# Mish feed-forward block on one core: x tiles 0 and 1 loaded one by one, w1's parts regrouped over two queues, tile 0 ahead of tile 1

## The chip, the core and the metric

One core of one Trainium2 chip runs the kernel. TensorE multiplies, VectorE (DVE) and ScalarE (ACT) read the products from PSUM, SyncE (SP) and ScalarE issue the DMAs, GpSimd (POOL) only builds an index table. The metric is the time of one execution on the device in microseconds (us). Three runs of the kernel before gave 105.01, 104.5 and 105.01 us, a median of 105.01.

## The reference

```python
B, S, D, F = 1, 2048, 512, 1792      # bfloat16
h = einsum("bsd,df->bsf", x, w1) + b1
sp = log1p(exp(-abs(h))) + where(h > 0, h, 0)
act = h * tanh(sp)                   # Mish
out = einsum("bsf,fd->bsd", act, w2)
```

## The kernel before

The 2048 rows of x are taken in four blocks of 512 (`BLOCKS`), a block being four tiles of 128 rows. The inner dimension D = 512 is four parts of 128, k = 0 to 3; F = 1792 is fourteen parts, f = 0 to 13. For each block the first half (`mm1`) makes, for each f, a PSUM bank of 128 x 512 from four products, one for each k, with a 128 x 128 piece of w1 as the weights and 512 columns of x transposed (`xT`) streaming; ScalarE then adds the bias, takes Mish and writes `a_sb` (`mish`, L159). The second half (`mm2`) makes, for each tile of rows, a bank from fourteen products over f; VectorE copies it to `o_sb` and SyncE stores it (`put`). Blocks go one after the other, and TensorE's order is the order in which the program is written.

There are eight banks of PSUM. In block 0, f uses bank (4 + f) % 8, so that f = 8 writes the bank that f = 0 wrote, and `mm1_step` makes TensorE wait for `free[bank]` ahead of an f's first product: there stands the token of whatever read the bank last.

Tiles of x come in two ways. Blocks 1 to 3 and tiles 2 and 3 of block 0 are transposed by the DMA on the way in (`t_xT`, `t_x23`). Tiles 0 and 1 are loaded as they lie (`x_nat`, one load of 256 rows, rows 2p and 2p + 1 in partition p) and transposed on TensorE by products with an identity (`transpose_x`, L145), copied from PSUM to `xT` by VectorE or ScalarE (L150).

The opening is what the change is about. TensorE first runs products on constants (`WARM`, L105), which need no load: 3200 columns in all. Then come the eight transposes and the first eight f of block 0 (`OPEN`), in an order written out by hand (L250 to L257): `first(fs, js, ks)` runs the products of these f, tiles js and parts k, k outermost. f 0 to 3 meet k 0 on tile 0 and then on tile 1, f 4 to 7 meet k 0 on both, then all eight f meet k 1 and 2 on tiles 0 and 1, then k 0 to 2 on tiles 2 and 3, and last k 3 on all four tiles, 512 columns wide. The last of each f starts its Mish.

Loads are issued by two engines, each in its order. ScalarE (L109): w1's part k 0, then k 2, for f 0 to 7. SyncE (L111 to L125): x's tiles 0 and 1, w1's k 1, then after a wait for the third product of `WARM` the DMA transpose of tiles 2 and 3, w1's k 3, b1, the rest of w1 (f 8 to 13), w2, and the DMA transposes of blocks 1 to 3. b1 is spread over partitions by VectorE (`spread_b1`, L246).

Of the kernel before, what the change touches and what calls it, by code (L numbers as in the profile page):

```python
# [4 lines left out]

P = 128
SQ = 32
WARM = (512,) * 5 + (256,) * 2 + (128,)
BLOCKS = (512, 512, 512, 512)


# [21 lines left out]
def bass_standalone__dense_activation_mish__prompt_kernel(  # L33
# [14 lines left out]
    KT, FT = D // P, F // P  # L48
    assert (S, D, F) == (2048, 512, 1792) and sum(BLOCKS) == S
    x2, out2 = x[0], out[0]  # L50
# [3 lines left out]
    OPEN = 8  # L54
    N0 = BLOCKS[0] // P

    with ExitStack() as es:
        def sb(name, shape, t):
            return es.enter_context(nc.sbuf_tensor(name, shape, t))

        x_nat = sb("x_nat", [P, 2, D], BF)
        xT = sb("xT", [P, KT, S], BF)
# [6 lines left out]
        ident = sb("ident", [P, P], BF)  # L69
        a_sb = sb("a_sb", [P, FT, S], BF)  # L70
        o_sb = sb("o_sb", [P, S // P, D], BF)
        ps = es.enter_context(nc.psum_tensor("ps", [P, 8, 512], F32))

        def sem(name):
            return es.enter_context(nc.semaphore(name))

        sp = Stream(nc.sync, None)
        pe = Stream(nc.tensor, sem("c_pe"))
        dve = Stream(nc.vector, sem("c_dve"))
        act = Stream(nc.scalar, sem("c_act"))  # L80
        pool = Stream(nc.gpsimd, sem("c_pool"))

        def load(q, dst, src, name, transpose=False):
            s = sem(name)
            (q.eng.dma_start_transpose if transpose else q.eng.dma_start)(dst, src).then_inc(s, 16)
            return (s, 16)

        def load_w1(q, ks, a, b):
            return load(q, w1_sb[:, ks, a * P:b * P], w1v[:, ks, a * P:b * P], "s_w1_%d_%d" % (ks.start, a))
# [6 lines left out]
        def load_part(q, k0, k1, a, b):  # L96
            t = load_w1(q, slice(k0, k1), a, b)
            for f in range(a, b):
                for k in range(k0, k1):
                    t_w1[k, f] = t  # L100

        t_bz = dve.mark(nc.vector.memset(b1_nat[:, :], 0.0))  # L102
        c_w = nc.const_aps.tensor(1.0, [P, P], BF)
        c_m = nc.const_aps.tensor(1.0, [P, 512], BF)
        t_fill = [pe.mark(nc.tensor.matmul(ps[:, 7, 0:n], c_w, c_m[:, 0:n], start=True, stop=True)) for n in WARM]  # L105

        act.eng.preload_act_table(ACT.Mish)  # L107
        act.wait(t_bz)
        for k in (0, 2):  # L109
            load_part(act, k, k + 1, 0, OPEN)  # L110
        t_xn = load(sp, x_nat[:, :, :], x2[0:2 * P, :].rearrange("(p j) d -> p j d", p=P), "s_xn")  # L111
        load_part(sp, 1, 2, 0, OPEN)
        sp.wait(t_fill[2])
        t_x23 = load(sp, xT[:, :, 2 * P:4 * P], x2[2 * P:4 * P, :], "s_x23", True)
        load_part(sp, 3, 4, 0, OPEN)
        sp.wait(t_bz)
        t_b1 = load(sp, b1_nat[0:FT, :], b1.rearrange("(j p) -> j p", p=P), "s_b1")
        load_part(sp, 0, KT, OPEN, FT)
        t = load(sp, w2_sb[:, :, :], w2v, "s_w2")
# [3 lines left out]
        for s in range(1, len(BLOCKS)):  # L123
            lo, hi = starts[s], starts[s + 1]
# [5 lines left out]
        t_id = dve.mark(nc.vector.tensor_scalar(ident[:, :], diff[:, :], 0, None, ALU.is_equal))  # L130

        free = [[] for _ in range(8)]
        t_cp = {(j, k): t_x23 for j in (2, 3) for k in range(KT)}
        t_mish = {}

        def transpose_x():

            pe.wait(t_xn, t_id)
            for bank, (eng, js, ks) in enumerate(((dve, (0,), (0,)), (act, (1,), (0,)), (dve, (0, 1), (1,)),
                                                  (act, (0, 1), (2, 3)))):  # L140
                n, m = len(ks), len(js)
                for i, k in enumerate(ks):
                    for h, j in enumerate(js):
                        lo = (i * m + h) * P
                        mm = nc.tensor.matmul(ps[:, bank, lo:lo + P], x_nat[:, j, k * P:(k + 1) * P], ident[:, :],  # L145
                                              start=True, stop=True)
                eng.wait(pe.mark(mm))
                dst = xT[:, ks[0]:ks[0] + n, js[0] * P:(js[-1] + 1) * P]
                src = ps[:, bank, 0:n * m * P].rearrange("p (k t) -> p k t", k=n)
                t = eng.mark(nc.vector.tensor_copy(dst, src) if eng is dve else act.eng.activation(dst, src, ACT.Copy))  # L150
                for k in ks:
                    for j in js:
                        t_cp[j, k] = t
                free[bank] = [t]

        def mish(s, f, bank, t_mm):
            n = BLOCKS[s]
            act.wait(t_b1c, t_mm)
            t = act.mark(act.eng.activation(a_sb[:, f, starts[s]:starts[s + 1]], ps[:, bank, 0:n], ACT.Mish,  # L159
                                            bias=b1_sb[:, f:f + 1]))  # L160
            t_mish[s, f] = t
            free[bank] = [t]

        def mm1_step(s, f, k, bank, js=None):

            n = BLOCKS[s]
            lo, hi = (0, n) if js is None else (js[0] * P, (js[-1] + 1) * P)
            first = k == 0 and lo == 0
            if first:
                pe.wait(*free[bank])  # L170
            pe.wait(t_w1[k, f])
            if s:
                pe.wait(t_xT[s])
            else:
                pe.wait(*[t_cp[j, k] for j in (js or range(N0))])
            return nc.tensor.matmul(ps[:, bank, lo:hi], w1_sb[:, k, f * P:(f + 1) * P],  # L176
                                    xT[:, k, starts[s] + lo:starts[s] + hi], start=first, stop=(k == KT - 1 and hi == n))
# [8 lines left out]

        def rows(i):

            if i < 2:
                return out2[0:2 * P, :].rearrange("(p j) d -> p j d", p=P)[:, i, :]  # L190
            return out2[i * P:(i + 1) * P, :]

        def mm2_step(i, f, lo, hi, bank):
# [7 lines left out]
        def put(i, lo, hi, bank, t_mm, q=sp):  # L201
            nonlocal n_out
            dve.wait(t_mm)
            t = dve.mark(nc.vector.tensor_copy(o_sb[:, i, lo:hi], ps[:, bank, 0:hi - lo]))  # L204
            free[bank] = [t]
            q.wait(t)
            q.eng.dma_start(rows(i)[:, lo:hi], o_sb[:, i, lo:hi]).then_inc(s_out, 16)
            n_out += 1
# [8 lines left out]
        def mm2_last(i):  # L217

            nonlocal n_out
            cuts = (0, D - 3 * P // 2, D - P // 2, D)  # L220
            toks = []
            for n, eng in enumerate((dve, dve, act)):
                lo, hi, bank = cuts[n], cuts[n + 1], (i + n) % 4
                for f in range(FT):
                    mm = mm2_step(i, f, lo, hi, bank)
                eng.wait(pe.mark(mm))
                dst, src = o_sb[:, i, lo:hi], ps[:, bank, 0:hi - lo]
                t = eng.mark(nc.vector.tensor_copy(dst, src) if eng is dve else act.eng.activation(dst, src, ACT.Copy))  # L228
# [12 lines left out]


        def spread_b1():
            dve.wait(t_b1)
            for j in range(P // SQ):
                t = dve.mark(nc.vector.transpose(b1_T[j * SQ:(j + 1) * SQ, :], b1_nat[:, j * SQ:(j + 1) * SQ]))  # L246
            dve.wait(t)
            return dve.mark(nc.vector.tensor_copy(b1_sb[:, :], b1_T[:, 0:FT]))  # L248

        transpose_x()  # L250
        t_b1c = spread_b1()
        first(range(4), (0,), (0,))
        first(range(4), (1,), (0,))
        first(range(4, OPEN), (0, 1), (0,))
        first(range(OPEN), (0, 1), (1, 2))
        first(range(OPEN), (2, 3), (0, 1, 2))
        first(range(OPEN), None, (3,), True)  # L257
        for f in range(OPEN, FT):
            mm1(0, f, (4 + f) % 8)

# [39 lines left out]
```

## Time and profile before

| | us |
|---|---|
| median of three runs | 105.01 |
| span of the profiled execution, first to last instruction | 104.0 |
| TensorE products busy | 101.4 (98% of the span) |
| weight loads busy (beside products) | 50.0 |
| ScalarE busy | 39.5 |
| VectorE busy | 13.2 |
| bytes moved by DMA | 7.94 MB |

The page gives no time of its own for the profiled execution other than the span. A busy share says how long an engine had at least one instruction under way; instructions on TensorE overlap, so that a product's duration is longer than the step from one to the next. In a row of the timeline the first number is the start in us from the span's first instruction, the second the length, then engine, line, operation, what is written and read, the shape and the count. SPq and ACTq are the DMA issues of SyncE and ScalarE; PEld is TensorE's weight load. The arrow in square brackets gives the idle time ahead of a row and what ended it. In the program's names w_sb stands for both `w1_sb` and `w2_sb`.

### The profile page before, as it was taken

To read this page: it belongs to the slowest core of one execution; us is meant where nothing else is said; L and a number is where in the kernel's file an instruction comes from. 1 tells how busy PE (TensorE), PEld (TensorE's weight loads), DVE (VectorE), ACT (ScalarE), POOL (GpSimd) and SP (SyncE) were. 2 spreads that over 40 slices of the span, in tenths; PEclk is the share of its full clock that TensorE was granted. 3 is DMA by queue.
4 is the path that set the end of the run, shared out by engine and by line. 5 is a ranking of instruction groups with operands and counts; after the bars stand their busy time and mean duration, and the time that the engine had idled before them with its cause. 6 is when DMAs were issued, how large, how long until landed. Compare 5 with 4: busy or idle time off the path is not lost.

```text
span 104.0 us, 1180 instructions
## 1 busy us (share of the span) xinstructions
PE 101.4 (98%) x520; PEld 50.0 (48%) x520; DVE 13.2 (13%) x26; ACT 39.5 (38%) x60; POOL 0.4 (0%) x5
## 2 busy tenths in 40 slices
PE   7999999999999999999999999999999999999993
PEld 2888444444444444444444444444444444444472
DVE  1212000112220000022220000022112000021241
ACT  4300899300027777200007777500005777700000
POOL 1000000000000000000000000000000000000000
PEclk9999999999999999999999999999999999999999
DMA  2999999991101000010111000001111000001111
GB/s 70 367 295 368 359 223 193 199 204 50 50 3 47 0 0 6 0 50 12 39 50 50 0 0 3 0 6 50 50 50 50 0 0 0 0 0 56 52 50 50
DMA packets 12833, 7.94 MB, mean 76 GB/s; under 512 B 7836, under 2 KB 12188, under 8 KB 12828
## 3 DMA queue, kind: packets, MB, share of 16 engines
q1 hardware_dynamic: 12396, 7.33, 26.8%
q10 hardware_dynamic: 432, 0.54, 1.5%
q8 instruction: 4, 0.07, 0.3%
q14 instruction: 1, 0.01, 0.0%
HBM read 3.94 MB, written 2.10 MB: 58 GB/s over the span
## 4 chain that ended last, share of the span: by engine, by line
PE 98%; ACT 0%; issue 0%
PE ps L176 47%; PE ps L198 47%; PE ps L105 3%; PE ps L145 1%; ACT o_sb L228 0%
## 5 line engine op out<-in xcount | busy, mean ns | idle before, releaser
L159 ACT ACTIVATE a_sb<-ps,b_sb 128x512 bf16<-128x512 f32 x56 | 37.1, 698 | 48.5 <-PE ps L176 48.5
L176 PE MATMUL ps<-xT,w_sb 128*128 128x512 bf16 (+2 forms) x252 | 50.0, 361 | 0.0
L198 PE MATMUL ps<-w_sb,a_sb 128*128 128x512 bf16 (+3 forms) x252 | 49.1, 355 | 0.0
L176 PEld LDWEIGHTS ps<-xT,w_sb 128*128 128x128 bf16 x252 | 25.0, 101 | 24.1
L198 PEld LDWEIGHTS ps<-w_sb,a_sb 128*128 128x128 bf16 x252 | 23.2, 98 | 25.6
L204 DVE CAST o_sb<-ps 128x512 bf16<-128x512 f32 x15 | 10.4, 692 | 80.8 <-PE ps L198 80.8
L228 ACT ACTIVATE o_sb<-ps 128x64 bf16<-128x64 f32 x1 | 0.2, 224 | 11.5 <-PE ps L198 11.5
L105 PE MATMUL ps<-const-bfloat16-1.0 128*128 128x512 bf16 (+2 forms) x8 | 2.8, 532 | 0.8 <-PEq L285 0.8
L105 PEld LDWEIGHTS ps<-const-bfloat16-1.0 128*128 128x128 bf16 x8 | 1.0, 136 | 2.2 <-issue 2.1
L150 ACT ACTIVATE xT<-ps 128x128 bf16<-128x128 f32 (+1 forms) x2 | 0.9, 438 | 2.2 <-PE ps L145 2.2
L107 ACT ACT_TABLE_LOAD x1 | 1.3, 1283 | 0.7 <-PEq L285 0.7
L246 DVE STREAM_TRANSPOSE b_T<-b_nat 32x32 bf16<-32x32 bf16 x4 | 0.8, 202 | 3.1 <-DMA b_nat<-in_b_dram 3.0
L145 PE MATMUL ps<-ident,x_nat 128*128 128x128 bf16 x8 | 1.0, 309 | 0.0
L150 DVE CAST xT<-ps 128x128 bf16<-128x128 f32 (+1 forms) x2 | 0.7, 358 | 2.5 <-PE ps L145 2.4
L228 DVE CAST o_sb<-ps 128x320 bf16<-128x320 f32 (+1 forms) x2 | 0.8, 392 | 1.5 <-PE ps L198 1.5
L145 PEld LDWEIGHTS ps<-ident,x_nat 128*128 128x128 bf16 x8 | 0.8, 138 | 0.2 <-DMA x_nat<-in_x_dram 0.2
L130 DVE TENSOR_SCALAR ident<-diff 128x128 bf16<-128x128 int32 x1 | 0.2, 227 | 0.2 <-POOL diff L128 0.2
L128 POOL IOTA diff<- 128x128 int32 x1 | 0.2, 234 | 0.4 <-POOLq L285 0.4
L102 DVE MEMSET b_nat<- 32x64 uint32 x1 | 0.1, 112 | 0.8 <-PEq L285 0.8
L248 DVE CAST b_sb<-b_T 128x14 f32<-128x14 bf16 x1 | 0.2, 176 | 0.0
L285 POOL MEMSET const-bfloat16-1.0<- 128x1 bf16 x1 | 0.1, 101 | 0.0
L285 POOL MEMSET const-uint8-127<- 128x1 uint8 x1 | 0.1, 101 | 0.0
(2 smaller groups left out, 0.2 us busy)
## 6 DMA issues: line engine op xcount, KB each, us to landing
out_dram<-o_sb SPq DMA_DIRECT2D x15, 128.0 KB, 1.7
w_sb<-in_w_dram SPq DMA_DIRECT2D x1, 1792.0 KB, 10.5
w_sb<-in_w_dram SPq DMA_DIRECT2D x1, 768.0 KB, 5.8
w_sb<-in_w_dram ACTq DMA_DIRECT2D x2, 256.0 KB, 3.7
w_sb<-in_w_dram SPq DMA_DIRECT2D x2, 256.0 KB, 3.6
x_nat<-in_x_dram SPq DMA_DIRECT2D x1, 256.0 KB, 2.6
out_dram<-o_sb SPq DMA_DIRECT2D x1, 112.0 KB, 1.7
xT<-in_x_dram SPq DMA_TRANSPOSE x4, 5.2
```

Of the source, the lines that this page charges most:

```text
L105: t_fill = [pe.mark(nc.tensor.matmul(ps[:, 7, 0:n], c_w, c_m[:, 0:n], start=True, stop=True)) for n in WARM]
L107: act.eng.preload_act_table(ACT.Mish)
L128: t_diff = pool.mark(pool.eng.iota(diff[:, :], pattern=[[1, P]], base=0, channel_multiplier=-1))
L130: t_id = dve.mark(nc.vector.tensor_scalar(ident[:, :], diff[:, :], 0, None, ALU.is_equal))
L145: mm = nc.tensor.matmul(ps[:, bank, lo:lo + P], x_nat[:, j, k * P:(k + 1) * P], ident[:, :], start=True, stop=True)
L150: t = eng.mark(nc.vector.tensor_copy(dst, src) if eng is dve else act.eng.activation(dst, src, ACT.Copy))
L159: t = act.mark(act.eng.activation(a_sb[:, f, starts[s]:starts[s + 1]], ps[:, bank, 0:n], ACT.Mish, bias=b1_sb[:, f:f + 1]))
L176: return nc.tensor.matmul(ps[:, bank, lo:hi], w1_sb[:, k, f * P:(f + 1) * P], xT[:, k, starts[s] + lo:starts[s] + hi], start=first, stop=( ...
L198: return nc.tensor.matmul(ps[:, bank, 0:hi - lo], a_sb[:, f, i * P:(i + 1) * P], w2_sb[:, f, lo:hi], start=(f == 0), stop=(f == FT - 1))
L204: t = dve.mark(nc.vector.tensor_copy(o_sb[:, i, lo:hi], ps[:, bank, 0:hi - lo]))
L228: t = eng.mark(nc.vector.tensor_copy(dst, src) if eng is dve else act.eng.activation(dst, src, ACT.Copy))
L246: t = dve.mark(nc.vector.transpose(b1_T[j * SQ:(j + 1) * SQ, :], b1_nat[:, j * SQ:(j + 1) * SQ]))
```

## The change

Tiles 0 and 1 become two loads of 128 rows in their plain order, both at the head of SyncE's queue; w1's k 0 and k 1 are issued by ScalarE, k 2 and k 3 by SyncE behind x; the DMA transpose of tiles 2 and 3 follows these without a wait for the warm-up. The warm-up has 2432 columns. Each tile has its own four transposes, k 0 copied by VectorE and k 1 to 3 by ScalarE in one copy, banks 0 and 1 for tile 0 and 2 and 3 for tile 1. Behind tile 0's transposes stand 384 columns on constants (`BRIDGE`), then f 0 to 3 meet k 0 on tile 0, and only then come tile 1's transposes. The order of the rest of the opening: f 4 and 5 on tile 0 and f 0 to 5 on tile 1 with k 0, f 6 and 7 on both, all f with k 1 to 3 on tiles 0 and 1, and at the end all f with k 0 to 3 on tiles 2 and 3.

```diff
-WARM = (512,) * 5 + (256,) * 2 + (128,)
+WARM = (512,) * 4 + (256, 128)
+BRIDGE = (256, 128)
...
+        def load_tile(q, j):
+            return load(q, x_nat[:, j, :], x2[j * P:(j + 1) * P, :], "s_xn%d" % j)
+
         act.eng.preload_act_table(ACT.Mish)
         act.wait(t_bz)
-        for k in (0, 2):
-            load_part(act, k, k + 1, 0, OPEN)
-        t_xn = load(sp, x_nat[:, :, :], x2[0:2 * P, :].rearrange("(p j) d -> p j d", p=P), "s_xn")
-        load_part(sp, 1, 2, 0, OPEN)
-        sp.wait(t_fill[2])
+        t_xn = [load_tile(sp, 0), load_tile(sp, 1)]
+        load_part(act, 0, 1, 0, OPEN)
+        load_part(act, 1, 2, 0, OPEN)
+        load_part(sp, 2, 3, 0, OPEN)
+        load_part(sp, 3, 4, 0, OPEN)
         t_x23 = load(sp, xT[:, :, 2 * P:4 * P], x2[2 * P:4 * P, :], "s_x23", True)
-        load_part(sp, 3, 4, 0, OPEN)
...
-        def transpose_x():
-
-            pe.wait(t_xn, t_id)
-            for bank, (eng, js, ks) in enumerate(((dve, (0,), (0,)), (act, (1,), (0,)), (dve, (0, 1), (1,)),
-                                                  (act, (0, 1), (2, 3)))):
-                n, m = len(ks), len(js)
+        def transpose_x(j):
+
+            pe.wait(t_xn[j], t_id)
+            for bank, ks, eng in ((2 * j, (0,), dve), (2 * j + 1, (1, 2, 3), act)):
+                n = len(ks)
                 for i, k in enumerate(ks):
...
-                dst = xT[:, ks[0]:ks[0] + n, js[0] * P:(js[-1] + 1) * P]
-                src = ps[:, bank, 0:n * m * P].rearrange("p (k t) -> p k t", k=n)
+                dst = xT[:, ks[0]:ks[0] + n, j * P:(j + 1) * P]
+                src = ps[:, bank, 0:n * P].rearrange("p (k t) -> p k t", k=n)
...
         def rows(i):
 
-            if i < 2:
-                return out2[0:2 * P, :].rearrange("(p j) d -> p j d", p=P)[:, i, :]
             return out2[i * P:(i + 1) * P, :]
...
-        transpose_x()
+        transpose_x(0)
+        for n in BRIDGE:
+            nc.tensor.matmul(ps[:, 7, 0:n], c_w, c_m[:, 0:n], start=True, stop=True)
+        first(range(4), (0,), (0,))
+        transpose_x(1)
         t_b1c = spread_b1()
-        first(range(4), (0,), (0,))
-        first(range(4), (1,), (0,))
-        first(range(4, OPEN), (0, 1), (0,))
-        first(range(OPEN), (0, 1), (1, 2))
-        first(range(OPEN), (2, 3), (0, 1, 2))
-        first(range(OPEN), None, (3,), True)
+        first((4, 5), (0,), (0,))
+        first(range(6), (1,), (0,))
+        first((6, 7), (0, 1), (0,))
+        first(range(OPEN), (0, 1), (1, 2, 3))
+        first(range(OPEN), (2, 3), range(KT), True)
```

More of the change, by code (lines that the diff above doesn't have):

```diff
@@ L134, in bass_standalone__dense_activation_mish__prompt_kernel @@
         t_mish = {}
-        def transpose_x():
-            pe.wait(t_xn, t_id)
-            for bank, (eng, js, ks) in enumerate(((dve, (0,), (0,)), (act, (1,), (0,)), (dve, (0, 1), (1,)),
-                                                  (act, (0, 1), (2, 3)))):
-                n, m = len(ks), len(js)
+        def transpose_x(j):
+            pe.wait(t_xn[j], t_id)
+            for bank, ks, eng in ((2 * j, (0,), dve), (2 * j + 1, (1, 2, 3), act)):
+                n = len(ks)
                 for i, k in enumerate(ks):
[L143 to L146, printed above, removed]
+                    mm = nc.tensor.matmul(ps[:, bank, i * P:(i + 1) * P], x_nat[:, j, k * P:(k + 1) * P], ident[:, :],
+                                          start=True, stop=True)
                 eng.wait(pe.mark(mm))
-                dst = xT[:, ks[0]:ks[0] + n, js[0] * P:(js[-1] + 1) * P]
-                src = ps[:, bank, 0:n * m * P].rearrange("p (k t) -> p k t", k=n)
+                dst = xT[:, ks[0]:ks[0] + n, j * P:(j + 1) * P]
+                src = ps[:, bank, 0:n * P].rearrange("p (k t) -> p k t", k=n)
                 t = eng.mark(nc.vector.tensor_copy(dst, src) if eng is dve else act.eng.activation(dst, src, ACT.Copy))
                 for k in ks:
-                    for j in js:
-                        t_cp[j, k] = t
+                    t_cp[j, k] = t
                 free[bank] = [t]
```

## The prediction

> **What bounds the kernel now.** First the chain of waits, the view that follows the end of the run back to its start. Columns: start, length, what.
>
> ```profile
> 0.77 2.82 PE ps L105 x8
> 3.60 0.85 PE ps L145 x8
> 4.45 13.01 PE ps L176 x84
> 17.46 12.09 PE ps L198 x56
> 29.55 12.09 PE ps L176 x56
> ```
>
> TensorE is the whole chain: warm-up (L105), transposes of x (L145), then products with no hole. A full half stage is 56 products of 512 columns in 12.09 us, 0.216 each, and nothing after 17.46 is touched. Block 0's first half takes 13.01, and what can be won is in there and in the 3.6 us ahead of it. Next the timeline of the opening, to see when work starts and how fast it goes.
>
> ```profile
> 1.58 1.48 PE L105 MATMUL ps<-const-bfloat16-1.0 128*128 128x512 bf16 x3
> ...
> 3.40 0.78 PEld L145 LDWEIGHTS ps<-ident,x_nat 128*128 128x128 bf16 x8 [0.18 <-DMA x_nat<-in_x_dram]
> 3.41 1.04 PE L145 MATMUL ps<-ident,x_nat 128*128 128x128 bf16 x8
> ...
> 3.74 0.74 DVE L150 CAST xT<-ps 128x128 bf16<-128x128 f32 x2 [2.42 <-PE ps L145]
> ...
> 4.25 1.06 PE L176 MATMUL ps<-xT,w_sb 128*128 128x128 bf16 x8
> ...
> 5.10 1.06 PE L176 MATMUL ps<-xT,w_sb 128*128 128x256 bf16 x4
> ...
> 6.13 1.36 PE L176 MATMUL ps<-xT,w_sb 128*128 128x256 bf16 x11
> ```
>
> The next rows group products by shape, the warm-up's of 2.2 to 2.5 us and the 256-column ones of 5.5 to 5.8 and of 6.4 to 6.7: count, busy time, mean ns of one.
>
> ```profile
> L105 PE MATMUL ps<-const-bfloat16-1.0 128*128 128x512 bf16 x3 | 1.5, 631 | 0.0
> ...
> L176 PE MATMUL ps<-xT,w_sb 128*128 128x256 bf16 x4 | 1.1, 418 | 0.0
> ...
> L176 PE MATMUL ps<-xT,w_sb 128*128 128x256 bf16 x6 | 0.8, 273 | 0.0
> ```
>
> A 256-column product takes 418 ns, then 273: at about 6.1 the array doubles its speed (the granted clock reads 1.00 on both sides, so only the durations show this). Steps from start to start: 512 columns cold (1.48 - 0.63) / 2 = 0.425; 256 cold (1.06 - 0.42) / 3 = 0.213; 128 cold 0.107 (eight from 4.25 end where 5.10 begins); 256 warm (1.36 - 0.27) / 10 = 0.109. A microsecond lost before 6.1 therefore costs half a microsecond at the end; one lost later costs all of itself. TensorE works without a break from 0.77 to 6.1, 5.3 us, before the clock rises. The tiles of x arrive (3.40) just as the warm-up ends.
>
> **The loads.** First the issues; then each load's size and its time from issue to landing, k 0, k 1 and k 3 in this order.
>
> ```profile
> 0.74 0.40 SPq L85 DMA_DIRECT2D x_nat<-in_x_dram  x1
> ...
> 0.95 0.86 ACTq L85 DMA_DIRECT2D w_sb<-in_w_dram  x2
> ...
> 1.20 0.41 SPq L85 DMA_DIRECT2D w_sb<-in_w_dram  x1
> ...
> 2.24 1.30 SPq L85 DMA_TRANSPOSE xT<-in_x_dram  x1
> ...
> 3.60 0.57 SPq L85 DMA_DIRECT2D w_sb<-in_w_dram  x1
> ```
>
> ```profile
> x_nat<-in_x_dram SPq DMA_DIRECT2D x1, 256.0 KB, 2.6
> w_sb<-in_w_dram ACTq DMA_DIRECT2D x1, 256.0 KB, 3.1
> w_sb<-in_w_dram SPq DMA_DIRECT2D x1, 256.0 KB, 3.6
> ...
> w_sb<-in_w_dram SPq DMA_DIRECT2D x1, 256.0 KB, 3.7
> ...
> xT<-in_x_dram SPq DMA_TRANSPOSE x1, 4.3
> ```
>
> And the bytes moved by stretch: the last column is GB/s.
>
> ```profile
> 1.60:2.00 0.40, 0.40 (x2) 0.13 (x1) 0.00 (x0) 0.40 (x1) 0.00 (x0) 1.00 0.59 108
> 2.00:2.40 0.40, 0.40 (x2) 0.15 (x1) 0.00 (x0) 0.02 (x1) 0.00 (x0) 1.00 0.64 200
> 2.40:2.80 0.40, 0.40 (x2) 0.15 (x1) 0.00 (x0) 0.00 (x0) 0.00 (x0) 1.00 0.96 328
> 2.80:3.20 0.40, 0.40 (x3) 0.27 (x2) 0.00 (x0) 0.00 (x0) 0.00 (x0) 1.00 0.95 343
> 3.20:3.60 0.40, 0.40 (x5) 0.22 (x4) 0.00 (x0) 0.00 (x0) 0.00 (x0) 1.00 1.06 389
> ```
>
> x lands at 0.74 + 2.6 = 3.34, k 0 at 0.95 + 3.1 = 4.05, k 1 at 1.20 + 3.6 = 4.80. Bytes moved: 43 KB by 2.0, 123 by 2.4, 254 by 2.8, 391 by 3.2, 547 by 3.6. x's 262 KB are through at 2.8, x and k 0 together (524) at 3.55, so a load's semaphore comes some 0.53 us behind its last byte. Which queue moves when is seen in the queues' shares of 3.0 to 3.4 us:
>
> ```profile
> q10 hardware_dynamic: 74, 0.15, 98.4%
> q1 hardware_dynamic: 1, 0.00, 4.0%
> ```
>
> q10 is ScalarE's, q1 SyncE's: k 0 has the engines nearly alone, though k 1 was issued on the other ring 2 us ago. With the landings 0.7 apart this reads as one load after the other in order of issue, across both rings.
>
> **The change, part by part.**
>
> *Loads.* The new order of issue is x 0 (SyncE 0.74), k 0 (ScalarE 0.95, where it was), x 1 (SyncE 1.14), k 1 (ScalarE, about 1.35), k 2 and k 3 (SyncE, 1.55 and 1.96), the DMA transpose (from about 2.4 for its 1.30), then b1 and the rest, all of which SyncE reaches some 0.4 us sooner than now since its wait on the warm-up is gone. Each 131 KB tile and each 262 KB part in turn over the byte counts above: x 0 through at 2.45, lands at 3.0; with rows half as long, which the early trace does not show, I take 3.05 (bounds: 2.8, where the warm-up ends, and 3.34, as the whole x now). x 0 and k 0 are 393 KB, through at 3.2: k 0 lands at 3.75. With x 1, 3.55: x 1 lands at 4.1. Then 0.7 each: k 1 at 4.8, k 2 at 5.5, k 3 at 6.3; the transpose, which now lands at 2.24 + 4.3 = 6.54 with k 3 behind it at 3.60 + 3.7 = 7.3, becomes the last of the same bytes, 7.3. Those that follow stay.
>
> *Warm-up.* 2432 columns in place of 3200 end at 0.77 + 2432 x 0.83 ns = 2.80. TensorE is then idle until x 0's first transpose at 3.05 + 0.05 = 3.10 (now 3.34 to 3.41).
>
> *Tile 0 first.* Four transposes 3.10 to 3.53, bridge of 384 columns 0.32, to 3.85. The copy that the first product needs is hidden by these: now it is 3.41 to 4.03 and the product needs it by 4.25, so 0.62 to 0.75 us are enough. k 0 lands at 3.75, 0.10 early. Four products of 128 columns: 3.85 to 4.28. Then tile 1's four transposes (x 1 is there since 4.1): 4.28 to 4.71; f 4 and 5 on tile 0: 4.92. Tile 1's six products of k 0 need VectorE's copy, 0.75 after 4.28, 5.03: a wait of 0.1 (bounds 0 and 0.11). Six by 0.107: 5.67. f 6 and 7 on both tiles, two by 0.213: 6.10. ScalarE's copies of k 1 to 3 (384 columns, between the two rows below) are over by 4.71 + 0.3 + 0.6 = 5.6 and free bank 3 in time.
>
> ```profile
> L150 ACT ACTIVATE xT<-ps 128x512 bf16<-128x512 f32 x1 | 0.6, 597 | 0.4 <-PE ps L145 0.4
> ...
> L150 ACT ACTIVATE xT<-ps 128x128 bf16<-128x128 f32 x1 | 0.3, 278 | 1.8 <-PE ps L145 1.8
> ```
>
> *Rest of the opening.* 24 products of k 1 to 3 on tiles 0 and 1, 32 of all k on tiles 2 and 3, 56 by 0.109 = 6.10: from 6.10, where the clock rises, to 12.20. k 1 is needed at 6.1, k 2 at 7.0, k 3 at 7.8, the transpose at 8.7: each load has 1.3 us or more to spare. The opening now has 70 products in place of 60 for the same columns; the ten more weight loads cost nothing, since the 128-column products above already run one load each at the full step of 0.107. Tiles 0 and 1 are also stored as plain rows now; the stores lie beside the later products, whose chain has no store in it, so nothing is put down for that.
>
> *The end of the opening.* Here the change adds a wait. Today:
>
> ```profile
> 10.39 0.81 PE L176 MATMUL ps<-xT,w_sb 128*128 128x512 bf16 x3
> ...
> 10.88 0.69 ACT L159 ACTIVATE a_sb<-ps,b_sb 128x512 bf16<-128x512 f32 x1 [5.79 <-PE ps L176]
> ...
> 10.88 2.42 ACT L159 ACTIVATE a_sb<-ps,b_sb 128x512 bf16<-128x512 f32 x4 [5.79 <-PE ps L176]
> ...
> 12.12 1.24 PE L176 MATMUL ps<-xT,w_sb 128*128 128x512 bf16 x5
> ```
>
> The last eight products, one for each f, are 512 wide and take 1.73 us, 10.39 to 12.12. f 0's Mish starts 0.11 behind its product's end, is over at 11.57, and so bank 4 is free 0.55 before f 8, at 12.12, writes it. After the change the last eight are 256 wide and take 0.87: they start at 12.20 - 0.87 = 11.33, f 0 is finished at 11.60, its Mish runs 11.71 to 12.40, and f 8 waits for bank 4 until 12.45 (0.05 as from x's landing to its use): 0.25 us at full price. Behind it in TensorE's order stands all the rest. f 9 needs the second Mish, (2.42 - 0.69) / 3 = 0.58 later, and comes 0.86 later, so only the first waits. All fourteen Mish end near 11.71 + 14 x 0.58 = 19.8; the second half needs the last at 12.45 + 5.18 + 2.8 = 20.4.
>
> **Sum.** The opening ends at 12.20 against 12.12, +0.08, and f 8 waits 0.25: +0.33. The shorter warm-up (0.32 us less of idle columns, worth 0.16) is eaten by the idle 0.3 before x 0, the 0.1 before tile 1 and the fine-grained order. The profiled span of 104.0 becomes 104.3. The median of the runs shown is 105.0, 1.0 above that span, which I carry over: 105.3.
>
> *A rule against the trace.* The Trainium skill (DMA: Bandwidth & Descriptors, "Queues, rings and completion order") says that each DMA engine takes turns between the rings that have work, packet by packet. The shares above show turns by whole loads instead, here. By the rule x 1 would share the engines with k 0, and the sum is that of the second rival.
>
> **Rivals.**
>
> *The first landings come late.* For: the first stretches move 108 and 200 GB/s against 389, and short rows or shared turns could keep x 0 until 3.34 and k 0 until 4.05 or 4.1. Against: the queues' shares. Then the first product starts at 3.41 + 0.75 = 4.16 in place of 3.85, 0.31 cold, 0.15 at the end: 105.45.
>
> *The clock rises later* (the other side). Place: TensorE's break from 2.80 to 3.10, where it had none. If what raises the clock counts unbroken work, it counts anew from 3.10, and 5.3 us later is 8.4: 2.3 us more at half speed, 1.15: 106.5. It decides once a break of 0.3 us counts. For: now there is no break at all ahead of the rise. Against: 0.3 in 5.3 is little, and the trace has no other break to judge by. The Trainium skill (TensorE: Matmul & The Clock Gate, "Part 1: The HAM clock gate") has free-running windows of 3.4 us of which one must be busy; by it, an estimate, the present rise would close a window begun at 2.7, and if the break spoils that one the rise moves to 9.5 and the time to 107.0. No run here shows which share is busy enough.
>
> *The wait for bank 4 is not there* (the change does what it is meant to, nothing is handed back): 105.1. Only if Mish started 0.25 earlier; the rows speak against it.
>
> *The clock rises earlier than it did in the profiled run*, at 4.3 in place of 6.1, for a reason that I don't see: 0.9 less, 104.4. The three runs, 104.5 to 105.01, leave room for some of this.
>
> **How the numbers follow.** Forecast 0.57 (own range 105.1 to 105.6, by the landing bounds), late landings 0.15, later clock 0.13, no wait 0.07, earlier clock 0.08. About 0.5%, 0.5 us, is what a measurement of this kernel can tell from no change; 105.53 is that line. Of the forecast 0.08 lies above it, of the late landings 0.07, of the later clock all: slower 0.28. Faster is the earlier clock, 0.08. Same: 0.64. The range leaves out the later clock's 106.5 and the earlier clock's 104.4 and takes in the runs' own half microsecond below and the landing bounds above: 104.5 to 106.1.
>
> **What would show it.** Right: transposes of tile 0 near 3.1; the first product of tile 0 near 3.85; a speed change near 6.1; a gap of some 0.25 us in TensorE ahead of the ninth f, ended by ScalarE's Mish, and none behind it. Wrong: 418 ns products of 256 columns beyond 6.5 (the clock), a gap ahead of the first product ended by a weight load (the rings), or the ninth f straight behind the eighth.

## The result, and the profile after

The changed kernel takes 105.97 us (median of 7 runs) against 104.99 for the kernel before (7 runs on the same chip): 1.0113 of it, with a 95% interval of 1.0083 to 1.0143. The forecast was 105.3, at most 0.5% above; the change costs 1.1%. The time lies inside the stated range of 104.5 to 106.1 by luck: the range was made for late first landings and the runs' own scatter, and neither is what happened. One of the seven runs, 107.97, is over 1.5% above the fastest and is left out of the ratio, as such runs are in every ratio below. The profiled execution took 106.44 us, its span is 105.1; the other five that count have spans of 104.3 to 104.8, so the profiled run is the slowest of those. In all 17 profiles of this document the products of the second half (L198 before, L195 after) take the same 84.65 us from the first start to the last, so whatever differs between two spans lies ahead of them.

First the chain of waits of the changed kernel (start, length, what), beside the five rows that the prediction shows of before:

```profile
1.36 5.45 DMA w_sb<-in_w_dram
6.81 0.05 issue
6.86 5.65 PE ps L175 x50
12.50 0.68 ACT a_sb L158
13.18 0.05 issue
13.22 5.35 PE ps L175 x24
18.58 12.09 PE ps L195 x56
30.66 12.09 PE ps L175 x56
```

Before, TensorE was the chain from 0.77 on. Now a load stands at its head: a part of w1, issued at 1.36 on ScalarE's ring, lands at 6.81, and everything before it on TensorE is no longer on the chain. Later a Mish (12.50 to 13.18) comes between the products: the first Mish, for which f 8 waits. Behind 13.22 the half stages take 12.09 us each, as before. The opening's timeline shows both waits in TensorE's rows, and three of the earlier ones:

```profile
2.96 0.61 PE L145 MATMUL ps<-ident,x_nat 128*128 128x128 bf16 x4
...
3.74 0.61 PE L175 MATMUL ps<-xT,w_sb 128*128 128x128 bf16 x4
4.37 0.61 PE L145 MATMUL ps<-ident,x_nat 128*128 128x128 bf16 x4
...
6.86 0.61 PE L175 MATMUL ps<-xT,w_sb 128*128 128x256 bf16 x4 [0.94 <-DMA w_sb<-in_w_dram]
...
12.22 1.40 PE L175 MATMUL ps<-xT,w_sb 128*128 128x256 bf16 x8
...
13.22 0.11 PEld L175 LDWEIGHTS ps<-xT,w_sb 128*128 128x128 bf16 x2 [0.36 <-ACT a_sb L158]
```

Tile 0 is transposed from 2.96 and its first product starts at 3.74, both 0.1 us sooner than forecast. Tile 1 is transposed at 4.37, 0.1 later than forecast. Then TensorE stands for 0.94 us, ended by w1's k 1. The wait for Mish ahead of f 8 shows on the weight loads (PEld) as 0.36; the last product of the eight begins at 12.87 in the trace, so that f 8 could have begun at 12.98 and begins at 13.22: 0.24.

f 8 begins 1.10 us later than in the profile of before (13.22 against 12.12). The step at k 1 is 1.22 us long in place of 0.11, so 1.11; bank 4 costs 0.24; the clock rises at 5.4 in place of 6.1, which gives back 0.35; 0.10 is left for the front. How late is k 1? The issues in the window about 1.36, with the median time from issue to landing, of the changed kernel:

```profile
w_sb<-in_w_dram ACTq DMA_DIRECT2D x1, 256.0 KB, 5.5
```

5.5 us from issue to landing; k 1, the second load of w1 then too, took 3.6 before. A load runs in 16 shares, and each adds one to its semaphore. Read from the trace's semaphore events, k 1's shares of the changed kernel have their median at 4.70 us, where the forecast had the whole load (4.8), and the last two at 6.52 and 6.81. The DMA records show two things. Most of its 2 KB packets take 84 ns, but two that start at 4.05 take 1179 and 818 ns. And the last fourteen of k 1's packets start some 160 ns apart in two rows (5.06, 5.22, 5.38 and so on, and 5.31, 5.47, 5.63 and so on), with a packet of SyncE's ring 80 ns behind each, where two packets of one load follow each other by 80. Read so, two engines have fallen behind, and on them k 1 takes turns with SyncE's loads, packet by packet. The records don't name a packet's engine; the turns are read from this spacing.

### The profile page after: what moved, and what is told of

The parts are those of the page before. It is cut to its first block, busy times and chain, and to the rows that moved or that the text cites. A ratio compares the mean times of both kernels' runs of the same rounds, so it can differ in the third digit from the quotient of the medians.

```text
span 105.1 us, 1201 instructions
## 1 busy us (share of the span) xinstructions
PE 101.4 (97%) x530; PEld 50.1 (48%) x530; DVE 13.1 (12%) x26; ACT 39.6 (38%) x60; POOL 0.4 (0%) x5
## 4 chain that ended last, share of the span: by engine, by line
PE 91%; DMA 5%; ACT 1%; issue 0%
PE ps L195 46%; PE ps L175 45%; DMA w_sb<-in_w_dram 5%; ACT a_sb L158 1%; ACT L111 1%; ACT o_sb L225 0%
## 5 line engine op out<-in xcount | busy, mean ns | idle before, releaser
L195 PE MATMUL ps<-w_sb,a_sb 128*128 128x512 bf16 (+3 forms) x252 | 49.1, 355 | 0.0
L195 PEld LDWEIGHTS ps<-w_sb,a_sb 128*128 128x128 bf16 x252 | 23.2, 98 | 25.6
L106 PE MATMUL ps<-const-bfloat16-1.0 128*128 128x512 bf16 (+2 forms) x6 | 2.2, 534 | 0.8 <-PEq L285 0.8
L150 ACT ACTIVATE xT<-ps 128x384 bf16<-128x384 f32 x2 | 1.0, 491 | 2.5 <-DVE xT L150 1.6
L150 DVE CAST xT<-ps 128x128 bf16<-128x128 f32 x2 | 0.6, 292 | 3.1 <-PE ps L145 3.1
L249 PE MATMUL ps<-const-bfloat16-1.0 128*128 128x256 bf16 (+1 forms) x2 | 0.5, 364 | 0.0
```

The costliest lines, as they stand in the source:

```text
L195: return nc.tensor.matmul(ps[:, bank, 0:hi - lo], a_sb[:, f, i * P:(i + 1) * P], w2_sb[:, f, lo:hi], start=(f == 0), stop=(f == FT - 1))
```

## The experiments

Times are medians; ratios are against runs of the kernel before on the same chip. "k 1" gives the median and the last share's landing, and "slow" the packets of 1 or 2 KB that started between 2.9 and 5.3 us and took over 400 ns, both read from the profiled run's records. SyncE issues k 1 in the old order of the loads, ScalarE in the new.

| | us | ratio (95% interval) | k 1 median, last | slow |
|---|---|---|---|---|
| before, first profile | 104.99 | | 4.61, 4.80 | 0 |
| before again | 104.69 | 0.9989 (0.9961 to 1.0017) | 4.64, 5.03 | 0 |
| changed, first profile | 105.97 | 1.0113 (1.0083 to 1.0143) | 4.70, 6.81 | 7 |
| changed again | 106.40 | 1.0123 (1.0075 to 1.0172) | 4.64, 5.42 | 2 |
| changed, old end | 106.06 | 1.0104 (1.0069 to 1.0138) | 4.68, 6.35 | 1 |
| before, new end | 105.20 | 1.0038 (1.0014 to 1.0063) | 4.66, 4.81 | 0 |
| before, new load order | 105.24 | 1.0043 (1.0011 to 1.0074) | 5.21, 5.44 | 0 |
| before, new front | 106.27 | 1.0117 (1.0066 to 1.0167) | 6.77, 6.92 | 9 |
| changed, transpose held | 106.24 | 1.0135 (1.0090 to 1.0180) | 4.75, 6.58 | 3 |
| changed, plain load for it | 106.54 | 1.0146 (1.0084 to 1.0207) | 5.73, 7.07 | 15 |
| before, x in two halves | 107.58 | 1.0185 (1.0124 to 1.0247) | 6.30, 6.54 | 6 |
| before, x in 1 KB rows | 105.27 | 1.0025 (0.9992 to 1.0059) | 4.72, 5.07 | 0 |
| changed, x in one load | 105.86 | 1.0100 (1.0065 to 1.0136) | 5.26, 5.48 | 0 |
| front alone, held | 105.75 | 1.0066 (1.0036 to 1.0096) | 5.90, 6.29 | 8 |
| before, k 0 in two halves | 108.32 | none formed | 5.09, 5.82 | 6 |
| changed, held | 105.38 | 1.0010 (0.9968 to 1.0052) | 4.49, 4.83 | 7 |
| changed, held, old end | 105.70 | 1.0072 (1.0040 to 1.0103) | 4.60, 4.90 | 5 |

The four runs of the kernel with k 0 in two halves differ by 2% among themselves (106.6 to 108.7), and no ratio was formed from them.

The last column counts in the window in which w1 moves, and its number alone doesn't say how late k 1 is. Outside the window, packets of 2 KB take over 400 ns in kernels with x in one load too: ahead of 2.9 us there are 8 in the second profile of before (up to 574 ns) and 14 in the changed kernel with x in one load. The rest of w1, too, has late shares in the kernel before (median 9.32, last 10.49), where f 8 needs it at 12.12 only. And with one slow packet, on SyncE's ring, k 1's last share comes at 6.35 (old end), with seven at 4.83 (held). The turns go better with late shares. Shares on ScalarE's ring (k 0 and k 1, in the old order k 0 and k 2) whose last packets come in two or more steps of some 160 ns stand in all eight profiles with an early load in two and w1's parts not held back, and in none of the six with both early loads whole nor of the two of the changed kernel with SyncE held. With both rings held they are on SyncE's ring, which has k 1 there.

**Controls: both kernels again.**

> The kernel before, unchanged, for the spans of its runs and a second profile. If the changed kernel's 0.3 us more around the span (106.44 - 105.1 = 1.34 against 105.01 - 104.0 = 1.05) belongs to the change, this one shows about 1.05 again in every run; if it varies by itself, some run here shows 1.3. Spans 103.5 to 104.1. Loads: k 0 to k 3 land within 0.2 us of the first profile (4.05, 4.8, 5.6, 7.3) if single slow transfers are rare; if they come at random in every run, one load is late by 0.5 us or more here too.

> The changed kernel, unchanged, for a second profile. Theory: the wait for k 1 (1.0 us in the first profile, two of 16 shares of that load landing 1.4 to 1.7 us behind the others) is chance and differs from profile to profile, between 0 and 1 us. Rival: it belongs to the order of the loads, and k 1 lands near 6.8 again, 2 us behind what the bytes ahead of it need.

The kernel before takes 1.3 to 1.4 us more than its span in every one of these runs (105.63 with 104.3, 104.41 with 103.1), as the changed kernel does. What lies around the span is the same for both; the first profile of before was an execution of some 105.3 us by this estimate, and the 1.0 of the prediction came from setting the median of other runs against its span. Its spans are the finding: 103.0 to 104.4 us in the 103 reference runs of these experiments, median 103.4. The first profile's 104.0 lies in the slower part. In the second profile the clock rises at 6.7 in place of 6.1, and the chain shows nothing else that differs:

```profile
4.45 13.32 PE ps L176 x84
17.78 12.09 PE ps L198 x56
```

13.32 in place of 13.01, half of the 0.6 us later rise. The Trainium skill (TensorE: Matmul & The Clock Gate, "Part 1: The HAM clock gate") has the gate judged over free-running windows of about 3.4 us, so that the rise differs from run to run; the profiles agree: 4.0 us (changed, again), 4.6 (before, new end), 5.4, 6.1, 6.7 and 6.9 (changed, old end), a width of 2.9. (The rise is read from where a product's step halves.)

The second profile of the changed kernel has k 1's last share at 5.42, so its lateness is chance in size; but it is late every time. Here it costs 0.15 us only (a step of 0.26 in place of 0.11). What f 8 waits for longest is the last share of the rest of w1, at 11.87 (the one before it came at 11.18):

```profile
12.01 0.59 PE L175 MATMUL ps<-xT,w_sb 128*128 128x512 bf16 x2 [0.26 <-DMA w_sb<-in_w_dram]
```

This was the fastest run of the changed kernel, 105.23; of the other three, 106.40 to 106.55, there is no profile. Two groups of products, of 4.85 to 5.05 us there and of 6.5 to 6.7 us in the kernel with the old end, show the early and the late clock:

```profile
L175 PE MATMUL ps<-xT,w_sb 128*128 128x128 bf16 x6 | 0.5, 221 | 0.1
```

```profile
L175 PE MATMUL ps<-xT,w_sb 128*128 128x256 bf16 x2 | 0.6, 407 | 0.2 <-DMA w_sb<-in_w_dram 0.2
```

221 ns for 128 columns is the fast array at 4.9 us already; 407 ns for 256 columns is the slow one at 6.6.

**The end of the opening, each way round.**

```diff
 # changed, old end (the other way round for: before, new end)
-        first(range(OPEN), (0, 1), (1, 2, 3))
-        first(range(OPEN), (2, 3), range(KT), True)
+        first(range(OPEN), (0, 1), (1, 2))
+        first(range(OPEN), (2, 3), (0, 1, 2))
+        first(range(OPEN), None, (3,), True)
```

> The changed kernel with the end of the opening as before (k 3 last on all four tiles, 512 columns wide), all else as changed. Theory: the changed kernel pays 0.25 us for bank 4, and this alone goes: 0.25 less than the changed kernel, 105.7, with f 8 straight behind f 7. Rival: the wait for bank 4 only stands in for time that the weights' late landing took already, and the time stays 105.9 to 106.0. Whatever k 1 costs is left as it is in both.

> The kernel before with only the new end of the opening (tiles 0 and 1 through k 3, then tiles 2 and 3 through k 3, 256 columns wide). Theory: 0.25 us slower than before, 105.25, a ratio of 1.0024, all of it a gap ahead of f 8 ended by ScalarE's Mish; k 3 is needed by about 8.8 and lands at 7.3. Rival: no gap, 105.0.

The kernel before with the new end is 0.38% slower, and the chain of its profile shows two waits and nothing else:

```profile
3.59 3.63 DMA w_sb<-in_w_dram
7.22 0.05 issue
7.27 3.90 PE ps L176 x34
11.17 0.68 ACT a_sb L159
11.84 0.05 issue
11.89 5.36 PE ps L176 x24
```

Mish ends at 11.84 and f 8 follows: the wait for bank 4, 0.24 us as in the changed kernel. The other is k 3, landing at 7.22, for which TensorE stood 0.22 us; the clock rose at 4.6 here, and the products came to k 3 at 7.05, not at the 8.8 that I had. Of that 1.0 was my own error (in this order k 3 is needed behind 16 products of 0.109 from about 6.1, at 7.8), and 0.75 is the earlier clock. The changed kernel with the old end is not measurably faster than with the new one (1.0104 against 1.0113, intervals that overlap), though no Mish stands in its chain any more. Its own profile waits for k 1 until 6.35. So this removal doesn't show the 0.25 us; the addition does.

**The load order alone, and the transpose.**

```diff
 # before, new load order
-        for k in (0, 2):
+        for k in (0, 1):
             load_part(act, k, k + 1, 0, OPEN)
...
-        load_part(sp, 1, 2, 0, OPEN)
-        sp.wait(t_fill[2])
+        load_part(sp, 2, 3, 0, OPEN)
+        load_part(sp, 3, 4, 0, OPEN)
         t_x23 = load(...)
-        load_part(sp, 3, 4, 0, OPEN)
 # changed, transpose held
+        sp.wait(t_xn[1])
         t_x23 = load(sp, xT[:, :, 2 * P:4 * P], x2[2 * P:4 * P, :], "s_x23", True)
 # changed, plain load for it
-        t_x23 = load(sp, xT[...], x2[2 * P:4 * P, :], "s_x23", True)
+        t_x23 = load(sp, xT[...], x2[2 * P:4 * P, :].rearrange("(p j) (a b) -> p (j a) b", p=P, b=2 * P), "s_x23")
```

> The kernel before with only the new order of the loads of w1 and of the DMA transpose (k 0, k 1 on ScalarE; x in one load, k 2, k 3, then the transpose on SyncE, without the wait for the warm-up). Theory: the order itself makes some of the 16 shares of k 1 late, as in the three profiles with it (last share at 6.81, 5.42 and 6.35, against 4.80, 5.03 and 4.81 with the old order): k 1 lands 0.5 to 2 us late here too, and the time is 0.5 to 1.0 us above the kernel before. Rival: the late shares come from x in two loads with rows of 1 KB, k 1 lands by 5.0 here, and the time is within 0.3 us of the kernel before.

> The changed kernel, with SyncE issuing the DMA transpose of tiles 2 and 3 only when tile 1 has landed (about 3.7 in place of 2.6). Theory: it is the issue of the transpose, 1.4 us long, beside the running loads of w1 that makes single packets take 0.3 to 1.2 us in place of 84 ns, from some 1.4 us after it begins; held back, k 1 lands by 5.0 and the slow packets move to 5.1 and later; the time falls by 0.3 to 0.8 us, towards 105.3 by the clock of the last runs. Rival: the slow packets come from w1's three parts standing in both rings at once, stay at 4.0 to 5.4, and the time stays 106.0 to 106.4.

> The changed kernel with the DMA transpose of tiles 2 and 3 replaced by a plain load of the same 256 KB in the same place, so that tiles 2 and 3 of the first block hold x untransposed. Theory as for the held transpose: without it k 1 lands by 5.0, no packet of k 1 or k 2 takes over 0.4 us, and the wait for k 1 in TensorE's order is gone or under 0.2 us. Rival (three parts of w1 in both rings at once): k 1's last share stays 0.5 us or more behind the others.

The two theories of that moment, the order of the loads and the issue of the transpose, fell. With the new order but x in one load, no share is late by itself: k 1 lands at 5.44, behind k 2 (4.77), because SyncE issues k 2 at 1.2, ahead of ScalarE's second load; its 16 shares lie within 0.4 us, and no packet of the window takes over 248 ns. The rival's numbers (k 1 by 5.0, within 0.3 us) didn't come either: the whole load is 0.4 to 0.6 us later than before, and the time is up by 0.4%. The profile, with the clock at 6.6, shows no wait for it; with a rise at 4.6, as in the kernel with the new end, k 1 would be needed at 5.3 to 5.4, so that an early clock exposes it by 0.1 to 0.2 us (an estimate, from that profile's products). Holding the transpose back or replacing it (by a load that leaves tiles 2 and 3 untransposed) leaves k 1 as late as in the changed kernel (6.58 and 7.07). The rival of these two, three parts of w1 in both rings at once, had the numbers right, but is not enough: the run with the new load order has the same three parts there and no late share. The transpose is not the cause; it is a victim: in the first profile of the changed kernel 19 of its packets start between 6.14 and 6.86 and end together at 7.3, once the last late share of w1 (k 2's, 6.98) is through.

**The front alone.**

```diff
 # before, new front = the changed kernel with the old end and
-        load_part(act, 1, 2, 0, OPEN)
-        load_part(sp, 2, 3, 0, OPEN)
-        load_part(sp, 3, 4, 0, OPEN)
+        load_part(act, 2, 3, 0, OPEN)
+        load_part(sp, 1, 2, 0, OPEN)
+        sp.wait(t_fill[2])
         t_x23 = load(sp, xT[:, :, 2 * P:4 * P], x2[2 * P:4 * P, :], "s_x23", True)
+        load_part(sp, 3, 4, 0, OPEN)
```

> The kernel before with only the new front: tiles 0 and 1 as own loads, the shorter warm-up and the bridge, tile 0 through k 0 ahead of tile 1; w1's parts, the transpose and the end of the opening as before. Theory: the front is worth about nothing (0.1 us less to 0.3 more than the kernel before: the transposes begin 0.35 us sooner, but tile 1 and bank 3 are waited for), and k 1 lands by 5.0. Rival: the front itself costs, 0.5 us or more.

The rival is right: the front itself costs 1.2%, as much as the whole change. But this kernel also changes an order that the changed kernel doesn't: with two loads of x ahead of it, SyncE issues k 1 at 1.66, behind ScalarE's k 2 (1.36), where before it was 1.20. All 16 shares of k 1 land between 6.60 and 6.92, behind a k 2 whose shares are spread from 4.51 to 6.72. How much of the 1.2% is this order and how much k 2's late shares, the run doesn't part. TensorE's row with the wait:

```profile
6.96 0.72 PE L176 MATMUL ps<-xT,w_sb 128*128 128x256 bf16 x5 [1.46 <-DMA w_sb<-in_w_dram]
```

**What of the front it is.** It holds one load more and rows of half the length; two runs part them, a third undoes the split in the changed kernel.

```diff
 # before, x in two halves
-        t_xn = load(sp, x_nat[:, :, :], x2[0:2 * P, :].rearrange("(p j) d -> p j d", p=P), "s_xn")
+        xv = x2[0:2 * P, :].rearrange("(p j) d -> p j d", p=P)
+        t_xn0 = load(sp, x_nat[0:P // 2, :, :], xv[0:P // 2, :, :], "s_xn0")
+        t_xn = load(sp, x_nat[P // 2:P, :, :], xv[P // 2:P, :, :], "s_xn")
 # before, x in 1 KB rows (the stores of tiles 0 and 1 follow)
-        t_xn = load(sp, x_nat[:, :, :], x2[0:2 * P, :].rearrange("(p j) d -> p j d", p=P), "s_xn")
+        t_xn = load(sp, x_nat[:, :, :], x2[0:2 * P, :].rearrange("(j p) d -> p j d", p=P), "s_xn")
 # changed, x in one load (the stores follow)
-        t_xn = [load_tile(sp, 0), load_tile(sp, 1)]
+        t_x01 = load(sp, x_nat[:, :, :], x2[0:2 * P, :].rearrange("(p j) d -> p j d", p=P), "s_xn")
+        t_xn = [t_x01, t_x01]
```

> The kernel before with x's first 256 rows in two loads of 128 KB, one for partitions 0 to 63 and one for 64 to 127, rows of 2 KB as before; TensorE waits for both. All else as before. Theory now: one more load ahead of w1's parts (four in place of three within the first 1.4 us, on two rings) is what makes packets of the later parts take 0.3 to 1.4 us: k 1 or k 2 has shares 0.5 us or more behind the others here, and x23 lands 0.5 us or more later than in the kernel before (6.6 to 6.8). Rival: it is the rows of 1 KB; then k 1 and k 2 land by 5.0 and 5.8 here and the time is within 0.2 us of the kernel before.

> The kernel before with x's first 256 rows in one load in which tile j holds rows 128 j and on, so 256 pieces of 1 KB in place of 128 of 2 KB; the output rows follow. All else as before. Theory (one more load): k 1 and k 2 land as before and the time is within 0.2 us of it. Rival (rows of 1 KB): k 1 or k 2 has shares 0.5 us or more late, and the time is above the kernel before as far as its order exposes them.

> The changed kernel with tiles 0 and 1 in one load with rows of 2 KB, as before; all else as changed, so tile 0 waits for the whole of x. Either way the split is undone: k 1's last share lands within 0.4 us of its median share, no wait of over 0.4 us for k 1; first transpose at 3.4 in place of 3.0. The time is 104.66 + 0.4 (end) + 0.3 (transpose late) = 105.3 to 105.5, 0.6 us under the changed kernel's 106.0 to 106.4. If the time stays at 106, the split isn't what costs.

Short rows leave no share late and cost 0.25%, not clear of nothing. Two halves with the old long rows make six slow packets; k 2's last three shares come at 6.28 to 6.34 with the other thirteen by 5.45, and k 1 lands at 6.54. The transpose lands at 7.38, 0.6 to 0.8 late, as the theory had it. Here the second half of x is late too, and TensorE stands ahead of its first transpose:

```profile
4.86 1.01 PE L147 MATMUL ps<-ident,x_nat 128*128 128x128 bf16 x8 [1.26 <-issue]
```

The last share of that half lands at 4.76, to which the profile gives no name (issue); before, all of x had landed at 3.36. All its shares are that late (4.41 to 4.76): it is issued at 1.36, behind k 0 (0.95). That wait, and the clock that rises at 7.9 behind it, is the time lost here; no product waits for the late shares of k 1 and k 2. The Trainium skill (DMA: Bandwidth & Descriptors, "Rules for kernel authors") advises against two transfers for two halves of the partitions, since they share the same engines and gain nothing; this run agrees, with the first half landed at 3.44 and the second at 4.76, and a loss of 1.9%.

The changed kernel with x in one load has no late share, as expected, but its time misses the forecast: 105.86, not 105.3 to 105.5. Its chain has other costs: the first transpose comes at 3.50, 0.7 us behind the shortened warm-up, the bridge still stands behind it, and f 8 waits for Mish. At 1.0100 against 1.0113 it is no faster than the changed kernel. With x whole SyncE also issues k 2 sooner, at 1.20 in place of 1.66 and ahead of k 1. So this run shows that late shares of k 1 go with the load in two or the issue times that come with it; it doesn't show that 0.6 us of the time come back without it.

**Holding the later loads.**

```diff
 # changed, held
         load_part(act, 1, 2, 0, OPEN)
+        sp.wait(t_xn[0])
         load_part(sp, 2, 3, 0, OPEN)
 # front alone, held: the wait for the warm-up dropped, and
+        act.wait(t_xn[0])
         load_part(act, 2, 3, 0, OPEN)
+        sp.wait(t_xn[0])
         load_part(sp, 1, 2, 0, OPEN)
 # before, k 0 in two halves: h = 0 and 1 on ScalarE's ring, TensorE waits for both
+            load(act, w1_sb[h * 64:h * 64 + 64, 0, 0:OPEN * P], w1v[h * 64:h * 64 + 64, 0, 0:OPEN * P], "s_k0_%d" % h)
 # changed, held, old end: the first of these and the old end of the opening
```

> The front alone (as in the run of that name: w1's order and the end as before), but k 1 on SyncE and k 2 on ScalarE are issued only when tile 0 has landed, at about 2.95, in place of 1.66 and 1.36; the wait for the warm-up is dropped. Theory (too many loads under way at once): no packet of k 1 or k 2 takes over 0.4 us, their 16 shares land within 0.5 us of each other, k 1 by 5.3, and the time comes down from 106.3 to between 104.4 and 105.0. Rival (a cut load does it, whatever is under way): shares late by 0.5 us or more again, time 106.

> The kernel before with k 0 in two loads of 64 partitions each on ScalarE's ring in place of x being cut; TensorE waits for both. Theory (one more load under way at once): k 1, k 2 or the second half of k 0 has shares 0.5 us or more behind their median, and the time is 0.5 us or more above the kernel before. Rival (it needs two loads at the head of SyncE's ring, or x itself): all shares of each load within 0.5 us, time within 0.4 us of the kernel before.

> The changed kernel with SyncE holding k 2 (and so k 3, the transpose and the rest) until tile 0 has landed, at about 2.95 in place of 1.66; nothing else. Theory: fewer loads under way while k 1 moves, so k 1's shares land within 0.5 us of each other and the wait for k 1 falls under 0.3 us; the end's 0.25 us stays; time 105.0 to 105.5. Rival: k 1 late by 0.5 us or more as in all profiles of the changed kernel, time 106.

> The changed kernel with both repairs: SyncE holds k 2 and what follows until tile 0 has landed, and the opening ends as before (k 3 last, 512 columns wide). Theory: both costs are gone, k 1's shares within 0.5 us of each other, no gap ahead of f 8 by Mish; the time is that of the kernel before, 0.997 to 1.002 of it, since the earlier tile 0 is worth 0.1 us at most. Rival: other late transfers (the rest of w1, one share 1.6 us late in the last profile) keep it 0.3% or more above; or the wait for bank 4 wasn't a cost of its own and the ratio is that of the held kernel, 1.001, or more.

Cutting k 0 in place of x makes late shares too: its first half's last share lands at 5.36, the median one at 4.19. Much of the time is lost to the order, though: the second half is issued at 1.56, behind k 1 (1.20), its median share lands at 5.73 and its last at 6.27, and the chain is

```profile
1.56 4.71 DMA w_sb<-in_w_dram
6.27 0.05 issue
6.32 14.20 PE ps L180 x84
```

So late shares need neither x nor SyncE's ring; either of the two early loads cut in two goes with them. One wait on SyncE in the changed kernel, which keeps its ring empty of k 2 and k 3 for longer, brings k 1's shares together (4.34 to 4.83) and the time back to 1.001 of the kernel before (0.9968 to 1.0052): most of the 1.1%. But it moves the slow packets rather than ends them. In the held kernel's timeline f 8 waits for the rest of w1, with one share at 12.28 (the others by 10.70):

```profile
12.41 0.38 PE L176 MATMUL ps<-xT,w_sb 128*128 128x512 bf16 x1 [0.39 <-DMA w_sb<-in_w_dram]
```

With the old end as well, the products need the transpose of tiles 2 and 3 a part earlier, where the new order of loads brings it last; it landed at 8.25, and the rest of w1 at 13.35:

```profile
8.30 0.94 PE L176 MATMUL ps<-xT,w_sb 128*128 128x256 bf16 x7 [0.28 <-DMA xT<-in_x_dram]
```

```profile
13.48 0.38 PE L176 MATMUL ps<-xT,w_sb 128*128 128x512 bf16 x1 [0.66 <-DMA w_sb<-in_w_dram]
```

It takes 0.7% more than the kernel before, though the profiled run, 106.7, was the slowest of twelve (median 105.70) and its waits are long ones. The rival of that run, other late transfers, is right, and so the two repairs don't add up: the new end belongs to the new order of loads, and the old end to the old one. The front alone with both rings held stays 0.7% slow: k 1, issued at 2.84 only, has its median share at 5.90 and its last at 6.29, with eight slow packets in its window, and is needed at 5.6.

No form tried is faster than the kernel before.

## Why the prediction was wrong

*The step that failed* is "each load has 1.3 us or more to spare". It took the landings from the bytes ahead of each load. For the median share that held (k 1 at 4.70, forecast 4.8); TensorE waits for the last of 16, and that came at 6.81, so that a wait of 1.11 us stands where the sum has nothing. k 2, k 3 and the transpose came late too (6.98, 7.49 and 8.51; forecast 5.5, 6.3 and 7.3). What goes with it is the early load cut in two: in the eleven profiles of kernels in which x or k 0 comes in two loads, one to fifteen packets take over 400 ns between 2.9 and 5.3 us, in the six of the others none; and in the changed kernel with x in one load, k 1's shares lie within 0.4 us. The first landings (2.92, 3.69 and 4.32 for tile 0, k 0 and tile 1; forecast 3.05, 3.75, 4.1) were nearly right, and these loads do go one after the other. The rival of late first landings (on the prediction's list the first, though its text calls it the second) had the wrong loads late. But the turns of the rings, packet by packet, which the prediction set aside by the rows of 3.0 to 3.4 us, are what k 1's late shares show. That the late k 1 is where the time goes in the changed kernel is shown by the profiled run (1.11 of 1.10 us net) and, for the median, by the held kernel; why one more load makes single packets slow and lets an engine fall behind, the runs don't show.

*The clock* was taken from one profile, 6.1 us, and its chance left at that. It differs by some 3 us from run to run, and a span of 103.4, the median of before, means a rise near 4.9 if nothing else differs (an estimate, by half a microsecond of span for one of the rise). That changes the sum in a way that I hadn't priced: the earlier the clock rises, the sooner the products come to each part of w1. The new end on the kernel before shows it, 0.22 us of waiting for k 3, which with a rise at 6.1 would have had some 0.6 to spare. A late clock hides late loads, and the profile that I argued from had one. The rival of a clock delayed by the short break didn't come about: with a break of some 0.3 us ahead of tile 0 the rises (4.0, 5.4 and 6.9) spread about those without (4.6, 6.1 and 6.7).

*The wait for bank 4* was right in place and size: 0.24 us measured twice, 0.25 forecast. *The earlier tile 0* was nearly right in its times, tile 1 being 0.1 late. *What lies around the span* was mis-sized, 1.0 for 1.3; it is the same in both kernels and changes nothing between them.

What stays open: the mechanism of the slow packets and what first puts an engine behind; whether it is the load more itself or the later issue that it gives to all behind it on its ring (some 0.5 us), which no run parts; and how the changed kernel's 1.1% divides. Alone on the kernel before, the new end costs 0.4%, the new load order 0.4% and the new front, with k 1 behind k 2, 1.2%; they overlap, since TensorE waits for the latest of several things.

## What to carry to other kernels

A load counts as landed with its last share, not when its bytes have been moved: in a profile of the changed form, look at the spread of the shares, and be slow to cut an early load in two for the sake of an earlier first tile, and try holding back the other ring's loads until the load that is needed next is through. Price the loads' slack for the fastest run of the engine that uses them, not for the one that was profiled: a late clock hides late loads. Halving the width of the last products before a bank is used again halves the time that the reader of that bank has.

## What the runs showed of the hardware

- Single DMA packets of 2 KB took up to 1.2 us in the changed kernel (1.7 with a plain load in place of the transpose) where the median is 84 ns.
- Shares of ScalarE's load that came late ended in 2 KB packets 160 ns apart, each with a packet of SyncE's ring 80 ns behind it, where packets of one load follow each other by 80 ns on an engine (the changed kernel, 5.06 to 6.31).
- Packets of a DMA transpose ended all at one instant: 19 packets of 256 bytes, started over 0.7 us, at about 7.3 in the changed kernel; 20 of the next transpose, started from 14.3 to 14.9, at about 15.5 in the kernel before, just ahead of w2's landing (15.55 to 15.64).
- Two profiles have long breaks in TensorE's work ahead of the rise: 1.6 us until 4.86 (x in two halves) and 2.1 us until 6.32 (k 0 in two halves). There the clock rose at 7.9 and 10.2, 3.0 and 3.9 us after work went on. Breaks of 0.3 us (the changed kernel: 4.0, 5.4, 6.9) show no such shift.
